# Attention, token mixing and FFT block: one product of zeros per attention step, theta's weights in two VectorE steps, mask copies and sink rows on GpSimd

## Chip, cores and metric

The kernel runs on one core of a Trainium2 chip. The metric is the device time of one execution in microseconds (us). The engines are TensorE (PE in the profile; PEld is its weight load), VectorE (DVE), ScalarE (ACT), GpSimd (POOL) and SyncE (SP, which here only issues DMAs). Each engine works through its own queue in order, and engines wait for each other by semaphores.

## The reference

Attention with a sliding window of 128 keys and 4 sink keys (2 batches, 8 heads, 768 positions, head size 64), then a block that turns each value by an angle and mixes the tokens, then a 2-D FFT's real part, a norm and an MLP. All inputs are f32.

```python
# attention, per batch and head; keep = first 4 keys, or the last 128 up to the query
a = softmax(where(keep, q @ k.T / 8, -1e9)); x = a @ v          # (2, 768, 512)
theta = x @ w_theta                                            # 512 x 512
zr, zi = x * cos(theta), x * sin(theta)
y = w_tok_r @ zr + w_tok_i @ zi                                # over the 768 tokens
u = x + y;  x = u + relu(u @ w_ch)
u = x + real(fft(fft(x, axis=1), axis=2))
out = u + relu(layernorm(u) @ w_ch1) @ w_ch2                   # 512 -> 2048 -> 512
```

The weights reach the kernel as 64-bit floating-point numbers, two 32-bit words each, and are converted to f32 on the chip.

## The kernel before

**Stages.** A first stretch (about 6 us) loads q, k, v and positions, and builds the first mask. Then comes attention (to about 140 us), token mixing of batch 0 and of batch 1 (`y_gen`), channel mixing and the Fourier transform (`ch_gen`, `dft_gen`), and the MLP in four chunks of three 128-row tiles (`mlp_gen`) to the end.

**Attention** (`attn_banded`) walks steps s. Tile n = s // 4 holds 128 queries of one batch, hp = s % 4 a pair of heads. At an even step the scores of four heads are multiplied (`score_mms`) and softmax runs on them (`scores`, L505): DVE adds the mask, writes scaled scores and the row minimum (L513), ACT takes the exponential (L517). The four score banks (tiles `sc` and `bank`) are reused by the next even step, so its products wait until ACT has read the last of them. One step later `turn` transposes the probabilities on PE (tile `tp`, L222), and ACT or DVE copies them to SBUF (L202, L203); three steps later `av` multiplies them by v (tile `oa`). `normalize` (L594 to L596) divides by the sums on DVE. From step 12 on, `theta_gen` multiplies a finished tile by theta's weights (tile `th`), 12 products a tile, spread over four steps; its end turns the result into a phase: ACT scales (L797), DVE rounds in two instructions (L798, L799), GpSimd subtracts (L800).

**Products of zeros.** In steps 1 to 11 (L630 to L638) PE multiplies a zero tile `z` into `th` twice per step; the results are not used.

**Masks** (`build_mask`, L415): `m0` to `m3` say what each kind of tile may see. Three DVE instructions per kind or fewer compute or copy them from the positions `win` (part of `xT`, which is reused later). `sink_v` (L468) spreads the sink rows of v over the heads, once per batch, on DVE.

**Conversion of weights** (`conv`, L263). A raw tile of 64-bit words arrives by DMA (three raw tiles, `raw`). ACT rescales the high words (L275). Then, if `low_act` is false, DVE works in three steps: shift the high word (L283), shift the low word and join (L284), put the sign in (L287). If `low_act` is true, ACT reduces the low word (L278) and DVE does two steps: L279 (shift and join) and L287. `low_act` is false until batch 1's token mixing and true after it. Theta's four weight tiles are converted in steps 5, 7, 9 and 11 (`THS`), and split into two f32r parts in steps 6, 8, 10 and 12 (ACT L202, GpSimd L207). From step 15 on the token-mixing weights follow (`P0B`).

**What sets the order.** The instructions are written in the order of the Python code, with hints such as "not before the last exponential" (`paced`, `after`). A scheduler with a simulated timeline then puts each engine's queue in order, so an edit in one place can move instructions in others.

Of the kernel before, what the change touches and what calls it, by code (L numbers as in the profile page):

```python
# [15 lines left out]
ALU = mybir.AluOpType  # L16
# [6 lines left out]
PW = 256 + SINK  # L23
BIG = 8.0e9
MAGIC = 12582912.0
# [17 lines left out]
P0B = 15  # L43
# [143 lines left out]
class _Body:  # L187
# [227 lines left out]
    def build_mask(self, n):  # L415

        nc, m = self.nc, self.masks
        win, key, sink = self.pos[:, 0:PW], self.pos[:, PW:PW + 128], self.pos[:, PW + 128:PW + 128 + SINK]
        a, s, z = slice(0, 128), slice(128, BLK), slice(BLK, PW)

        def drop(o, x, k):
            nc.vector.tensor_scalar(o, x, self.val[:, k:k + 1], -BIG, op0=ALU.is_ge, op1=ALU.mult)

        if n == 0:
            drop(key, key, 0)
            drop(win, win, 1)
            nc.vector.tensor_tensor(m[0], win[:, z], key, op=ALU.max)
        if n == 1:
            nc.vector.tensor_tensor(m[1][:, a], win[:, a], key, op=ALU.max)
            nc.vector.tensor_copy(m[1][:, 128:PW], win[:, 128:PW])  # L430
        if n == 2:
            drop(win[:, s], sink, 0)
            nc.vector.tensor_copy(m[2], win)
        if n == 3:
            for o, w in ((a, z), (s, s), (z, a)):
                nc.vector.tensor_copy(m[3][:, o], win[:, w])


    def pairs(self, what, n):
# [27 lines left out]

    def sink_v(self, b):  # L468
        vs = self.take(H, D)
        self.nc.vector.tensor_tensor(  # L470
            vs,
            self.ks[b][1].rearrange("p (o d) -> p o d", o=1).to_broadcast([128, H, D]),
            self.hm.rearrange("p (h o) -> p h o", o=1).to_broadcast([128, H, D]),
            op=ALU.mult,
        )
        self.vs[b] = vs
# [128 lines left out]
    def attn_banded(self):  # L605
        last = len(self.seq) - 1
        nc = self.nc
# [5 lines left out]
        for s in range(nstep + T0 + AL + 4):  # L613
# [16 lines left out]
            if 0 < s < first(0):  # L630

                ref = self.pe
                for _ in range(2):
                    i = nc.tensor.matmul(  # L634
                        self.zth[:, 0:256], lhsT=self.zz[:, 0:128], rhs=self.zz, start=s == 1, stop=False,
                        skip_group_check=True,
                    ).ins
                    self.after(i, ref)  # L638
# [24 lines left out]
            if n < last:  # L663
                if s in MST:
                    with self.paced(ref=self.last_exp):
                        self.build_mask(1 + MST.index(s))
                if s == SKS:
                    with self.paced(ref=self.last_exp):
                        self.sink_cols(0, 0, 1, 2)
                if hp == 0:  # L670
                    if n == 1:
                        with self.paced():
                            self.sink_v(0)
                    elif n and self.seq[n][1] == 0:
                        self.sink_cols(b, 0, 1)
                        self.sink_v(b)
            if s in THS:
                self.pump(0, lag=0, ref=self.last_exp)
            elif s - 1 in THS:
                with self.paced(ref=self.last_exp):  # L680
                    self.weight_split("th", THS.index(s - 1))
            elif P0B <= s < P0E and s % P0N == 0:
                self.pump(12, lag=0, ref=self.last_exp)
# [89 lines left out]
    def theta_gen(self, b, i):  # L773
        nc = self.nc
        x = self.x[b, i]
        tp = self.ps_tp.next().rearrange("p (a m) -> p a m", a=4)
        for a in range(4):
            self.tr(tp[:, a, :], x[:, a * 128:(a + 1) * 128], self.ident)
        hi = self.take(4, 128, dt=F32R)
        lo = self.take(4, 128, dt=F32R)  # L780
        self.rnd("a", hi, tp)
        xt = self.xT[b][:, :, i * 128:(i + 1) * 128]
        nc.scalar.activation(xt, tp, AF.Copy)
        self.low("v" if 6 * b + i >= ETH else "p", lo, xt, hi)
        self.tl = nc.cur_bb.bb.instructions[-1]
        yield
        th = self.ps_th.next()
        for a in range(4):
            wh, wl = self.ws["th", a]
            self.mm(th, hi[:, a, :], wh, a == 0, False)  # L790
            self.mm(th, hi[:, a, :], wl, False, False)
            self.mm(th, lo[:, a, :], wh, False, a == 3)
            if a < 3:
                yield
        self.give(hi, lo)
        ph, km = self.take(512), self.take(512)
        nc.scalar.activation(ph, th, AF.Copy, scale=INV2PI)  # L797
        nc.vector.tensor_scalar(km, ph, MAGIC, None, op0=ALU.add)  # L798
        nc.vector.tensor_scalar(km, km, MAGIC, None, op0=ALU.subtract)  # L799
        nc.gpsimd.tensor_tensor(ph, km, ph, op=ALU.subtract)  # L800
        self.give(km)
        self.ph[b, i] = ph
        yield
# [568 lines left out]
```

## Time and profile before

| what | value |
|---|---|
| median of 3 runs | 604.54 us (604.18 to 605.95) |
| the profiled execution | 604.34 us |
| its span in the trace | 602.6 us |
| PE busy | 587.1 us (97%) |
| DVE, ACT busy | 343.9 and 344.0 us (57% each) |
| POOL busy | 301.6 us (50%) |
| chain that ended last | PE 85%, DVE 8%, ACT 4% |

The span is what the trace covers; 1.7 us of the execution's time lie around it. Matmul ends are modelled, so PE's 97% means "something was always queued on PE", not that it worked at its peak. The chain that ended last follows the work back from the last instruction to what released it each time; an engine's share of it in a stretch says which engine the stretch waited for.

### The profile page before, as it was taken

To read this page: it belongs to the slowest core of one execution; us is meant where nothing else is said; L and a number is where in the kernel's file an instruction comes from. 1 tells how busy PE (TensorE), PEld (TensorE's weight loads), DVE (VectorE), ACT (ScalarE), POOL (GpSimd) and SP (SyncE) were. 2 spreads that over 40 slices of the span, in tenths; PEclk is the share of its full clock that TensorE was granted. 3 is DMA by queue.
4 is the path that set the end of the run, shared out by engine and by line. 5 is a ranking of instruction groups with operands and counts; after the bars stand their busy time and mean duration, and the time that the engine had idled before them with its cause. 6 is when DMAs were issued, how large, how long until landed. Compare 5 with 4: busy or idle time off the path is not lost.

```text
span 602.6 us, 9514 instructions
## 1 busy us (share of the span) xinstructions
PE 587.1 (97%) x3486; PEld 516.3 (86%) x3486; DVE 343.9 (57%) x711; ACT 344.0 (57%) x775; POOL 301.6 (50%) x252
## 2 busy tenths in 40 slices
PE   8989999999989999989999999999999999999996
PEld 6867888887878899968999999998998899998995
DVE  5776688868999678973566776465334211121112
ACT  4576666777864555556678784437447444344340
POOL 1121322144775542517655745659757565665651
PEclk9999999999999999999999999999999999999998
DMA  8842443200334314610066640100001000010001
GB/s 268 302 140 70 127 131 112 78 13 2 104 106 161 112 52 121 194 35 2 1 198 199 196 142 1 54 1 0 1 0 54 2 0 1 1 52 1 1 1 59
DMA packets 23336, 46.60 MB, mean 77 GB/s; under 512 B 2512, under 2 KB 9552, under 8 KB 23280
## 3 DMA queue, kind: packets, MB, share of 16 engines
q1 hardware_dynamic: 21744, 43.46, 22.8%
q0 software_dynamic: 1248, 2.17, 1.3%
q8 instruction: 29, 0.48, 0.3%
q10 hardware_dynamic: 288, 0.28, 0.1%
q14 instruction: 27, 0.22, 0.1%
HBM read 42.75 MB, written 3.15 MB: 76 GB/s over the span
## 4 chain that ended last, share of the span: by engine, by line
PE 85%; DVE 8%; ACT 4%; issue 1%; DMA 1%; POOL 1%; SPq 0%; ACTq 0%; DVEq 0%; POOLq 0%
PE pc L217 26%; PE acc L217 22%; PE s L217 9%; PE bank L217 8%; PE oa L217 6%; PE th L217 5%; PE tp L222 4%; PE sc L217 3%; PE s L222 2%; ACT t L202 1%; DVE t L207 1%; PE th L634 1%; ACT p L517 1%; DMA xT<-in_q_dram 1%; DVE t L818 1%
## 5 line engine op out<-in xcount | busy, mean ns | idle before, releaser
L207 POOL TENSOR_TENSOR t<-t 128x512 fp32r<-128x512 f32 x151 | 202.2, 1361 | 169.0 <-ACT t L202 143.6
L217 PE MATMUL acc<-t 128*128 128x512 f32 x648 | 178.5, 394 | 0.0
L202 ACT ACTIVATE t<-t 128x512 fp32r<-128x512 f32 x172 | 101.9, 625 | 71.5 <-PE acc L217 26.5
L217 PEld LDWEIGHTS acc<-t 128*128 128x128 f32 x648 | 116.5, 188 | 17.9
L217 PE MATMUL pc<-t 128*128 128x384 f32 (+1 forms) x672 | 124.8, 314 | 1.0 <-POOL t L207 0.6
L217 PEld LDWEIGHTS pc<-t 128*128 128x128 f32 x672 | 113.9, 188 | 10.9 <-POOL t L207 0.8
L1132 DVE SCALAR_TENSOR_TENSOR t<-pc,t 128x384 fp32r<-128x384 f32 x64 | 35.6, 557 | 123.4 <-ACT t L1131 122.1
L207 POOL TENSOR_TENSOR t<-xT,t 128x512 fp32r<-128x512 f32 x39 | 52.7, 1369 | 58.8 <-ACT t L202 27.2
L217 PE MATMUL s<-t 128*128 128x256 f32 (+3 forms) x492 | 70.6, 286 | 1.6 <-DVE st L1052 0.8
L217 PE MATMUL pc<-uh,t 128*128 128x384 f32 x256 | 70.6, 337 | 0.0
L217 PEld LDWEIGHTS s<-t 128*128 128x128 f32 x492 | 65.7, 190 | 5.0 <-DVE st L1052 1.0
L217 PE MATMUL bank<-t 128*128 128x512 f32 x216 | 65.7, 400 | 2.1 <-DVE t L207 1.6
L1131 ACT ACTIVATE t<-pc 128x384 fp32r<-128x384 f32 x64 | 31.3, 489 | 59.8 <-PE pc L217 57.1
L275 ACT ACTIVATE raw<-raw 128x512 f32<-128x512 f32 x58 | 38.9, 675 | 14.9 <-DMA raw<-in_w_ch_dram 13.2
L217 PEld LDWEIGHTS bank<-t 128*128 128x128 f32 x216 | 38.8, 188 | 9.6 <-DVE t L207 3.2
L217 PEld LDWEIGHTS pc<-uh,t 128*128 128x128 f32 x256 | 46.2, 188 | 0.8
L217 PE MATMUL pc<-ul,t 128*128 128x384 f32 x128 | 43.1, 336 | 0.6 <-DVE ul L207 0.6
L517 ACT ACTIVATE p<-sc,nb 128x272 f32<-128x272 f32 (+1 forms) x72 | 33.1, 466 | 15.4 <-DVE nb L513 14.9
L217 PE MATMUL oa<-t 128*128 128x64 f32 x288 | 39.3, 266 | 0.0
L217 PEld LDWEIGHTS oa<-t 128*128 128x128 f32 x288 | 37.2, 192 | 2.2 <-DVE t L203 0.7
L217 PE MATMUL th<-t 128*128 128x512 f32 x132 | 37.8, 416 | 0.0
L800 POOL TENSOR_TENSOR t<-t 128x512 f32<-128x512 f32 x12 | 17.1, 1421 | 36.9 <-DVE t L799 31.0
(145 smaller groups left out, 836.3 us busy)
## 6 DMA issues: line engine op xcount, KB each, us to landing
raw<-in_w_ch_dram SPq DMA_DIRECT2D x36, 512.0 KB, 4.2
kst<-in_k_dram SPq DMA_DIRECT2D x12, 256.0 KB, 4.0
raw<-in_w_tok_rT_dram SPq DMA_DIRECT2D x6, 512.0 KB, 3.5
raw<-in_w_tok_iT_dram SPq DMA_DIRECT2D x6, 512.0 KB, 3.6
out_dram<-t SPq DMA_DIRECT2D x12, 256.0 KB, 2.1
t<-in_q_dram SPq DMA_DIRECT2D x10, 256.0 KB, 5.1
t<-in_v_dram SPq DMA_DIRECT2D x10, 256.0 KB, 4.8
raw<-in_w_theta_dram SPq DMA_DIRECT2D x4, 512.0 KB, 6.5
```

The source lines that it names most:

```text
L202: return nc.scalar.activation(o, i, AF.Copy).ins
L207: e.tensor_tensor(o, x, hi.bitcast(F32), op=ALU.subtract)
L217: i = self.nc.tensor.matmul(o, lhsT=lhsT, rhs=rhs, start=start, stop=stop, skip_group_check=True).ins
L222: self.chained(self.nc.tensor.transpose(o, x, ident).ins)
L275: nc.scalar.activation(hf, hf, AF.Copy, scale=2.0 ** -112)
L517: self.last_exp = nc.scalar.activation(p[:, h, 0:wd], sc[:, 0:wd], AF.Exp, bias=nb[:, h:h + 1], scale=-1.0, accum_out=sm[:, h:h + 1]).ins
L634: i = nc.tensor.matmul(self.zth[:, 0:256], lhsT=self.zz[:, 0:128], rhs=self.zz, start=s == 1, stop=False, skip_group_check=True,).ins
L800: nc.gpsimd.tensor_tensor(ph, km, ph, op=ALU.subtract)
L818: self.tm = e.tensor_tensor(t, x, t, op=ALU.mult).ins
L1131: nc.scalar.activation(hh, hp, AF.Relu)
L1132: self.hl = nc.vector.scalar_tensor_tensor(hl, in0=hp, scalar=0.0, in1=hh.bitcast(F32), op0=ALU.max, op1=ALU.subtract).ins
```

## The change

- The loop that issues products of zeros runs once per step instead of twice: 11 products instead of 22.
- `low_act` is set to `s < P0B` in each attention step. P0B is 15, so theta's four weight tiles take the form with ACT's L278 and DVE's L279 and L287; the token weights from step 15 on are converted as before.
- The plain copies of the masks `m1`, `m2` and `m3` (five instructions) and both `sink_v` products go to GpSimd. The computed parts of the masks stay on DVE.
- The rounding of the phase, adding and subtracting MAGIC, becomes one DVE instruction (12 tiles).

```diff
@@ build_mask
-            nc.vector.tensor_copy(m[1][:, 128:PW], win[:, 128:PW])
+            nc.gpsimd.tensor_copy(m[1][:, 128:PW], win[:, 128:PW])
...
-            nc.vector.tensor_copy(m[2], win)
+            nc.gpsimd.tensor_copy(m[2], win)
...
-                nc.vector.tensor_copy(m[3][:, o], win[:, w])
+                nc.gpsimd.tensor_copy(m[3][:, o], win[:, w])
@@ sink_v
-        self.nc.vector.tensor_tensor(
+        self.nc.gpsimd.tensor_tensor(
@@ attn_banded
-                for _ in range(2):
+                for _ in range(1):
                     i = nc.tensor.matmul(
...
+            self.low_act = s < P0B
             if s in THS:
@@ theta_gen
-        nc.vector.tensor_scalar(km, ph, MAGIC, None, op0=ALU.add)
-        nc.vector.tensor_scalar(km, km, MAGIC, None, op0=ALU.subtract)
+        nc.vector.tensor_scalar(km, ph, MAGIC, MAGIC, op0=ALU.add, op1=ALU.subtract)
```

The scheduler's order changes in attention on PE, DVE, ACT, POOL and SP; behind the first third of batch 0's token mixing all queues of the executed branch stand in the same order as before. Lines behind L676 move down by one in the changed kernel (L797 becomes L798); the rounding keeps the number L799.

On DVE, at tile 1's second softmax and the first conversion of a theta weight (`raw_108`); `nb_172` and `sm_175` belong to tile 1, `nb_173` to tile 2. Before:

```order
L203 COPY t<-tp_199 128x256
L283 TENSOR_SCALAR t<-raw_108 128x512
L284 SCALAR_TENSOR_TENSOR t<-raw_108,t 128x512
L287 SCALAR_TENSOR_TENSOR t<-raw_108,t 128x512
L513 ISA sc_197,nb_172<-sc_197,m_187 128x272
L513 ISA nb_172 128x1
L513 ISA sc_196,nb_172<-sc_196,m_187 128x272
```

After:

```order
L203 COPY t<-tp_199 128x256
L279 SCALAR_TENSOR_TENSOR t<-raw_108 128x512
L513 ISA sc_197,nb_172<-sc_197,m_187 128x272
L513 ISA nb_172 128x1
L287 SCALAR_TENSOR_TENSOR t<-raw_108,t 128x512
L513 ISA sc_196,nb_172<-sc_196,m_187 128x272
```

One conversion step instead of three stands ahead of tile 1's second softmax.

On DVE, between tile 1's last and tile 2's first softmax, where the second theta weight (`raw_109`) is converted. Before:

```order
L594 TENSOR_SCALAR rs_178<-sm_175 128x8
L595 RECIPROCAL rs_178<-rs_178 128x8
L596 TENSOR_TENSOR t<-oa_200,rs_177 128x512
L203 COPY t<-tp_199 128x512
L283 TENSOR_SCALAR t<-raw_109 128x512
L284 SCALAR_TENSOR_TENSOR t<-raw_109,t 128x512
L513 ISA bank,nb_173<-bank,m_188 128x272
L513 ISA nb_173 128x1
L513 ISA sc_195,nb_173<-sc_195,m_188 128x272
```

After:

```order
L596 TENSOR_TENSOR t<-oa_200,rs_177 128x512
L203 COPY t<-tp_199 128x512
L594 TENSOR_SCALAR rs_178<-sm_175 128x8
L595 RECIPROCAL rs_178<-rs_178 128x8
L513 ISA bank,nb_173<-bank,m_188 128x272
L513 ISA nb_173 128x1
L513 ISA sc_195,nb_173<-sc_195,m_188 128x272
L513 ISA nb_173 128x1
L279 SCALAR_TENSOR_TENSOR t<-raw_109 128x512
L287 SCALAR_TENSOR_TENSOR t<-raw_109,t 128x512
```

The normalizing product L596 and the copy L203 no longer stand behind L594, which waits for the last exponential's sum, and the conversion has moved behind two of the four score instructions.

On ACT, the same place: the second theta weight between tile 1's and tile 2's exponentials. Before:

```order
L517 ACTIVATE p_184,sm_175<-bank,nb_172 128x272
L202 ACTIVATE t<-t 128x512
L275 ACTIVATE raw_109<-raw_109 128x512
L202 ACTIVATE t<-tp_198 128x512
L517 ACTIVATE p_183,sm_176<-bank,nb_173 128x272
```

After:

```order
L517 ACTIVATE p_184,sm_175<-bank,nb_172 128x272
L202 ACTIVATE t<-t 128x512
L275 ACTIVATE raw_109<-raw_109 128x512
L278 ACTIVATE raw_109<-raw_109,below 128x512
L202 ACTIVATE t<-tp_198 128x512
L517 ACTIVATE p_183,sm_176<-bank,nb_173 128x272
```

L278 is new there, ahead of the copy and of the next four exponentials.

## Rows read from the trace of the kernel before

**Rows 1.** Stages: start:end, length, each engine's busy us, PE's granted clock, DMA.

```profile
5.00:21.00 16.00, 15.11 (x102) 11.75 (x103) 11.72 (x54) 10.19 (x42) 0.30 (x1) 1.00 1.00 351
21.00:38.00 17.00, 15.56 (x117) 12.71 (x113) 14.60 (x42) 9.67 (x32) 3.52 (x3) 1.00 0.58 182
...
80.00:133.00 53.00, 53.00 (x370) 42.55 (x370) 40.32 (x131) 38.77 (x122) 15.89 (x13) 1.00 0.25 79
133.00:180.00 47.00, 44.86 (x264) 37.65 (x263) 43.75 (x58) 35.99 (x63) 29.71 (x20) 1.00 0.22 68
```

**Rows 2.** Chain shares by line, 21 to 38 us, then 80 to 133 us.

```profile
by line: ACT p L517 16.1%; DVE t L283 13.3%; DVE sc L513 12.4%; DVE t L284 12.3%; DVE t L203 10.5%; issue 7.4%; DVE t L596 7.3%; DVE t L287 6.6%; DVE bank L513 4.2%; DVE t L470 4.0%; ACT raw L275 3.4%; ACT t L202 3.1%; DVE nb L513 2.9%; DVE
...
by line: PE oa L217 30.9%; PE th L217 27.3%; PE tp L222 20.7%; PE sc L217 15.0%; PE bank L217 6.3%
```

**Rows 3.** Products of zeros: ns min/median/max, first and last start.

```profile
L634 PE MATMUL th<-z x44: 379/379/483, 6.6 to 30.8; 128*128 128x256 f32 x44
```

**Rows 4.** Chain in order of time: start us, us, what.

```profile
6.87 1.52 ACT p L517 x8
...
13.03 1.06 PE th L634 x4
```

**Rows 5.** First theta load: issue in the timeline, then us to landing.

```profile
8.79 1.31 SPq L251 DMA_DIRECT2D raw<-in_w_theta_dram  x3
...
raw<-in_w_theta_dram SPq DMA_DIRECT2D x1, 512.0 KB, 6.1
```

**Rows 6.** Timeline, 15 to 36 us: start, us, engine, what, [idle before].

```profile
15.01 0.67 ACT L275 ACTIVATE raw<-raw 128x512 f32<-128x512 f32 x1
...
17.52 0.44 DVE L513 CUSTOM_DVE_ANT_0 sc<-sc,m 128x272 f32<-128x272 f32 x1
...
21.00 0.59 ACT L202 ACTIVATE t<-tp 128x512 f32<-128x512 f32 x1
...
22.89 0.44 DVE L513 CUSTOM_DVE_ANT_0 bank<-bank,m 128x272 f32<-128x272 f32 x1
...
23.49 0.49 ACT L517 ACTIVATE p<-bank,nb 128x272 f32<-128x272 f32 x1 [1.90 <-DVE nb L513]
...
25.79 0.63 ACT L202 ACTIVATE t<-t 128x512 fp32r<-128x512 f32 x1
...
26.50 1.27 POOL L207 TENSOR_TENSOR t<-t 128x512 fp32r<-128x512 f32 x1 [4.53 <-ACT t L202]
...
27.01 1.04 DVE L283 TENSOR_SCALAR t<-raw 128x512 int32<-128x512 int32 x1 [1.31 <-ACT raw L275]
...
30.62 0.49 ACT L517 ACTIVATE p<-sc,nb 128x272 f32<-128x272 f32 x1 [3.16 <-DVE nb L513]
...
35.94 0.49 ACT L517 ACTIVATE p<-bank,nb 128x272 f32<-128x272 f32 x1 [1.57 <-DVE nb L513]
```

**Rows 7.** The two-step conversion where it runs later: L278 and L279.

```profile
L278 ACT ACTIVATE raw<-raw,below x33: 734/754/784, 205.8 to 360.9; 128x512 int32<-128x512 uint32 x33
...
L279 DVE SCALAR_TENSOR_TENSOR t<-raw x9: 676/685/1799, 206.6 to 252.7; 128x512 int32<-128x512 int32 x9
```

**Rows 8.** DVE instructions that the change removes or moves, by line.

```profile
L798 DVE TENSOR_SCALAR t<-t x12: 410/425/925, 46.2 to 166.9; 128x512 f32<-128x512 f32 x12
...
L470 DVE TENSOR_TENSOR t<-vsr,hm x2: 681/682/684, 11.5 to 29.4; 128x512 f32<-128x512 f32 x2
...
L433 DVE COPY m<-xT x1: 295/295/295, 10.3 to 10.3; 128x272 f32<-128x272 f32 x1
```

**Rows 9.** Timeline of DVE in batch 0's token mixing.

```profile
162.94 1.78 DVE L287 SCALAR_TENSOR_TENSOR t<-raw,t 128x512 int32<-128x512 int32 x1
...
166.95 0.93 DVE L798 TENSOR_SCALAR t<-t 128x512 f32<-128x512 f32 x1
```

**Rows 10.** The last microseconds, columns as in rows 1.

```profile
598.00:600.00 2.00, 0.00 (x0) 0.00 (x0) 0.00 (x0) 0.00 (x0) 0.00 (x0) 0.67 0.61 220
600.00:601.00 1.00, 0.00 (x0) 0.00 (x0) 0.00 (x0) 0.00 (x0) 0.00 (x0) 0.50 0.07 20
```

## The prediction, made before the changed kernel ran

> **What bounds the kernel now.** I read the windows of the stages first, then the chain that ended last inside each, and only then single rows. The stages show four regimes. In the opening of attention (5 to 21 us) the DMA engines are busy all the time (share 1.00) and PE is busy as well, but part of that is products of zeros. From 21 to 38 us VectorE is the fullest engine, 14.60 of 17 us, and the chain there is made of exponentials and of VectorE's conversion steps L283, L284 and L287; matmuls hardly stand in it [rows 1, 2]. From 80 to 133 us the chain is PE alone. From 133 to 180 us, the turn to token mixing, VectorE is busy 43.75 of 47 us and PE waits for it [rows 1, 2]. Behind that PE sets the end, and all queues stand in the same order before and after. So a change in the first 180 us shifts what follows as a whole: what attention and the turn gain, the end gains.
>
> **Term A: attention's opening, to 36 us.** Two things are removed here, products of zeros and VectorE work, and one is added on ScalarE.
>
> A product of zeros is two matmul rows (44 rows for 22 products), and a pair of products takes 1.06 us of the chain [rows 3, 4]. Halving them frees 11 x 0.53 = 5.8 us on PE if PE were what everything waits for. It is not. The first group stands beside eight exponentials that hold the chain for 1.52 us [rows 4], so nothing comes of it. Later groups are on the chain until tile 1 (13.03 us), and PE gets about 1.6 us ahead by its second scores. But then the queues meet the first theta load, which no product of zeros moves: issued at 8.79 us, 6.1 us to landing, so it lands at 14.9 us, and ACT's L275 started on it at 15.01 us [rows 5, 6]. So I follow ACT and DVE from that landing, by four points.
>
> Point 1, the second softmax of tile 1 on DVE, at 17.52 us before [rows 6]. In the new order one conversion step stands ahead of it, not three, but L278 stands ahead of that. From 14.9 us: L275 0.67, L278 0.75, L279 0.69, with 0.1 for signals, gives 17.1 us [rows 6, 7]. That is 0.4 earlier; the 1.6 us of PE are cut to this.
>
> Point 2, the first exponential of tile 2, at 23.49 us before, 1.90 us of it spent waiting for DVE, which had L594 to L596, a copy, L283 and L284 ahead of its L513 at 22.89 [rows 6]. In the new order L596 and the copy no longer stand behind L594's wait, and L279 stands behind two of the score instructions. So ACT is what remains. Its queue is as before with one L278 more: the copy that began at 21.00 begins at 21.00 - 0.4 + 0.75 = 21.35, takes 0.59, and the exponential comes at 22.0. That is 1.5 earlier.
>
> Point 3, the second softmax of tile 2, exponential at 30.62 us before, after waiting 3.16 us [rows 6]. ACT takes 2.3 us from its first exponential to the next L202 (23.49 to 25.79). So 22.0 + 2.3 = 24.3, then L202 0.63, L275 0.67, L278 0.75 give 26.35, L279 0.69 gives 27.05, and a score instruction and its exponential (0.6, from 22.89 to 23.49) 27.7. That is 2.9 earlier. It contains sink_v's 0.68 us on DVE, which stood here ahead of the scores [rows 8], and the slow L283 of 1.04 us [rows 6].
>
> Point 4, tile 3's first exponential, at 35.94 us before. From 27.7: 2.3 for the exponentials, 0.63 + 0.67 + 0.75, and two copies of at most 0.59 give 33.2, that is 2.7 earlier; one L283 less among the scores behind it makes about 0.3 more. **A = -3.0 us.**
>
> Bounds of A. The far end is PE's, -5.8. The near end comes from GpSimd. The mask copies cost DVE at most 0.30 us each and sink_v 0.68 us [rows 8]; what they cost on GpSimd no row shows, and the nearest row is a product of the same size, 1.27 us [rows 6]. Nobody waits for them directly: the masks m2 and m3 are first used by tile 2 and later (behind 20 us), m1 at 12 us. But they run beside DVE. An L283 that began while GpSimd's product of 26.50 us ran took 1.04 us, and in token mixing an L287 took 1.78 us where its like takes 0.69 [rows 6, 7, 9]. If both sink_v products hit a conversion step like that, 2 x 1.1 = 2.2 us come back and A is -0.8. I take -3.0, since the copies fall into 6 to 12 us, ahead of the conversions, and only one sink_v meets them.
> The Trainium skill speaks against the move here: SBUF — State Buffer, section "Who interferes with whom", says that GpSimd and VectorE share a pair of ports, and that when VectorE reads two tensors from SBUF, or runs in its mode with both ports, whichever comes second waits for the first to finish. The rows just named agree; by that rule every one of the seven moved instructions may stop VectorE once, and A would be the -0.8 of the near end.
>
> **Term B: attention from 36 to 133 us.** Eight of the twelve roundings lie here, 0.42 us each on DVE [rows 8], and the scheduler has set score products ahead of theta's products in several places, which gives softmax more cover. The chain is PE alone [rows 2], and PE's work is the same, so I book nothing: **B = 0**. For bounds I take the weight load's idle time, 53 - 42.55 = 10.5 us [rows 1]: PE's rows hide waits in there, a fifth of which may be won or lost by a new order, so -2 to +2.
>
> **Term C: the turn to token mixing, 133 to 180 us.** DVE is full here and PE waits for its splits. Two roundings' first halves (L798) lie in the full stretch, a usual one of 0.42 us and one stretched to 0.93 us [rows 8, 9], and the queues around them are unchanged, so what is taken out comes off the end of the stretch: **C = -1.3 us**. Bounds: 0, if GpSimd's products then meet DVE elsewhere; -2.2, with two more roundings in the 133 to 143 us tail.
>
> **Sum.** -3.0 + 0 - 1.3 = -4.3 us. The profiled execution took 604.34 us (span 602.6 and 1.7 around it), so the changed one takes 600.0; the median of the runs stands 0.2 above the profiled execution: **600.2 us**. The bounds together give 604.34 - 9.9 to 604.34 + 1.2; they will not all fall to one side.
>
> **Rivals.**
> 1. More than forecast: the new order lets PE run closer to its own work in attention (B = -2), or A comes nearer to PE's end. Then about 597. For it: softmax has more cover in the new order. Against: the chain names nothing but PE. Chance 0.13.
> 2. The gain is covered: the conversions on ACT and DVE, with GpSimd in the way, hold the opening (A = -0.8). With B and C that gives 604.5 - 2.1 = 602.4. For it: the added L278 stands ahead of exponentials four times, 3.0 us of ACT. Against: ACT is busy 9.67 of 17 us in 21 to 38 [rows 1]. Chance 0.15. This is also the case in which the removed products do nothing, since PE then waits for softmax instead.
> 3. The lead is given back: attention ends 3 us earlier, but in a worse order, and C's stretch begins with another GpSimd and DVE overlap (A + B = 0). Then 603.2. Chance 0.12.
> 4. Slower: TensorE's clock. The granted clock is 1.00 in every stage [rows 1]; that is the 2.4 GHz level. It falls only behind the last matmul, with PE at rest, to 0.67 and then to 0.50, the 1.2 GHz level [rows 10]. The products of zeros fill pauses of PE, and half of them go. If the clock fell for the stretch from 15 to 35 us, PE's work there (15.56 us busy of 17, less 4 x 0.53 of zeros, about 13.4 per 17 us [rows 1, 4]) would run at half speed, so 20 us of it lose 10, and the sum is -4.3 + 10: 610. It decides from about 9 us at the low level on, where half of the time lost eats the gain. Against: PE still has work in four fifths of the time. Chance 0.10.
> The Trainium skill has this as a rule, TensorE: Matmul & The Clock Gate, section "HAM oscillation — how this bites in real kernels": pauses of PE bring its clock to half, and the products behind each pause start slow. The trace agrees at its end and shows no fall inside the program.
>
> **How the numbers follow.** My forecast, 598.3 to 602.3, has 0.50; rivals 1 to 4 have 0.13, 0.15, 0.12 and 0.10. The range leaves out rival 4 and the lower half of rival 1: 596.5 to 604.2. What a measurement of this kernel can tell from no change is about 0.3%, 1.8 us, so faster means below 602.7. The forecast, rival 1 and most of rival 2 are faster: 0.50 + 0.13 + 0.09 = 0.72. The rest of rival 2, and rival 3 but for 0.01, are the same: 0.17. Rival 4 and that 0.01 are slower: 0.11.
>
> **What would show it.** Point by point in the changed trace: the first L275 still near 15 us (if earlier, the load was not what held it); the second softmax of tile 1 near 17.1, the exponentials of points 2 to 4 near 22.0, 27.7 and 33.2; PE in the same order of work about 3 us earlier at 80 to 133 us; the end of DVE's full stretch about 4.3 us earlier, near 175 instead of 180; from there on the same distances as before. I am wrong on A if those exponentials move by under 1 us or by over 5, on B if the lead at 133 us differs from that at 36 us by over 2 us, on C if it does not grow by about 1 us to 180 us, and wholly if the granted clock shows a stretch below 1.00 ahead of the end.

## The result, and the profile after

The changed kernel takes 599.91 us (median, 599.74 to 600.28) against 604.65 us (604.18 to 605.95): a ratio of 0.9917 [0.9905, 0.9929], so 4.7 us or 0.8% faster. The forecast of 600.2 us lies 0.3 us off, and the gain is well beyond the 0.3% that a measurement can tell. The profiled execution took 599.92 us, 4.4 less than the one before.

The stage windows of the changed kernel, which answer to [rows 1] (start:end, length, busy us of PE, PEld, DVE, ACT, POOL, then PE's granted clock, DMA share, GB/s):

```profile
5.00:21.00 16.00, 14.11 (x91) 9.58 (x89) 10.97 (x47) 10.73 (x42) 2.77 (x7) 1.00 0.99 353
21.00:38.00 17.00, 16.15 (x130) 13.61 (x130) 13.33 (x44) 14.30 (x45) 6.33 (x5) 1.00 0.65 219
...
80.00:133.00 53.00, 52.61 (x370) 43.11 (x369) 34.86 (x113) 36.73 (x112) 15.49 (x13) 1.00 0.21 66
133.00:180.00 47.00, 46.06 (x265) 38.99 (x264) 42.49 (x59) 32.79 (x60) 28.55 (x19) 1.00 0.24 74
```

In the first stage PE is busy 1.0 us less. In the second DVE falls from 14.60 to 13.33 us and ACT rises from 9.67 to 14.30. In the last DVE falls from 43.75 to 42.49 and PE rises from 44.86 to 46.06. The granted clock is 1.00, the 2.4 GHz level, in all four.

The four points of term A, from the timeline of the changed kernel; they answer to [rows 6]:

```profile
15.14 0.68 ACT L275 ACTIVATE raw<-raw 128x512 f32<-128x512 f32 x1
15.70 0.75 ACT L278 ACTIVATE raw<-raw,below 128x512 int32<-128x512 uint32 x1
...
16.48 0.70 DVE L279 SCALAR_TENSOR_TENSOR t<-raw 128x512 int32<-128x512 int32 x1 [1.76 <-ACT raw L278]
...
17.10 0.44 DVE L513 CUSTOM_DVE_ANT_0 sc<-sc,m 128x272 f32<-128x272 f32 x1
...
22.20 0.50 ACT L517 ACTIVATE p<-bank,nb 128x272 f32<-128x272 f32 x1
...
28.09 0.49 ACT L517 ACTIVATE p<-sc,nb 128x272 f32<-128x272 f32 x1 [0.77 <-DVE nb L513]
...
32.89 0.50 ACT L517 ACTIVATE p<-bank,nb 128x272 f32<-128x272 f32 x1
```

Forecast were 17.1, 22.0, 27.7 and 33.2; the lead over the kernel before is 0.4, 1.3, 2.5 and 3.05 us. The waits at points 2 and 3, 1.90 and 3.16 us before, are gone and 0.77 us. Times count from the first instruction of each execution; the first exponential of all comes at 6.87 us before and at 7.30 us after, so a few tenths between two executions say little.

The end of attention and the end of DVE's full stretch are read on PE: the first product into `pc` opens the long run of token mixing, and a matmul of L217 into `bank` gets the last split that comes late (the second part of a value, made by DVE's L207). First the kernel before, then the changed one, both from the timeline:

```profile
150.03 0.52 PE L217 MATMUL pc<-t 128*128 128x256 f32 x3
...
179.69 0.51 PE L217 MATMUL bank<-t 128*128 128x512 f32 x1 [1.15 <-DVE t L207]
```

```profile
146.55 0.52 PE L217 MATMUL pc<-t 128*128 128x256 f32 x3
...
175.38 0.50 PE L217 MATMUL bank<-t 128*128 128x512 f32 x1 [0.28 <-DVE t L207]
```

The lead is 3.5 us at the first of the two places and 4.3 us at the second, as summed. In between it is not steady. The first exponential of a softmax comes 4.2 us earlier at 36.4 us, 9.9 earlier at 69.1 and 6.4 earlier at the last softmax (122.1). The last product of attention with the sink rows (PE, into `oa`) comes only 2.4 earlier, at 142.86 instead of 145.28, but there the order differs: six products into `bank` stand ahead of it, not two, so it is no measure of PE's lead. So the numbers fit; whether the reasons do is what the experiments ask.

### The profile page after: what moved, and what is told of

It reads as the page before. It is cut to its first block, busy times and chain, and to the rows that moved or that the text cites. A ratio compares the mean times of both kernels' runs of the same rounds, so it can differ in the third digit from the quotient of the medians.

```text
span 598.1 us, 9446 instructions
## 1 busy us (share of the span) xinstructions
PE 583.1 (97%) x3464; PEld 512.8 (86%) x3464; DVE 332.8 (56%) x688; ACT 344.0 (58%) x779; POOL 305.4 (51%) x259
## 4 chain that ended last, share of the span: by engine, by line
PE 63%; DVE 5%; ACT 1%; POOL 1%; issue 1%; POOLq 0%; ACTq 0%
PE pc L217 25%; PE acc L217 21%; PE s L217 9%; PE bank L217 7%; PE s L222 2%; POOL t L207 1%; DVE t L207 1%; ACT t L202 1%; DVE t L1145 0%; DVE t L818 0%; DVE t L986 0%; DVE t L998 0%; DVE t L1001 0%; ACT t L1067 0%; DVE t L1052 0%
## 5 line engine op out<-in xcount | busy, mean ns | idle before, releaser
L207 POOL TENSOR_TENSOR t<-t 128x512 fp32r<-128x512 f32 x151 | 203.3, 1366 | 151.5 <-ACT t L202 124.6
L217 PE MATMUL acc<-t 128*128 128x512 f32 x648 | 178.5, 394 | 0.0
L217 PEld LDWEIGHTS acc<-t 128*128 128x128 f32 x648 | 116.5, 188 | 17.9
L217 PE MATMUL pc<-t 128*128 128x384 f32 (+1 forms) x672 | 124.9, 314 | 1.0 <-POOL t L207 0.6
L217 PEld LDWEIGHTS pc<-t 128*128 128x128 f32 x672 | 113.9, 188 | 10.9 <-POOL t L207 0.8
L207 POOL TENSOR_TENSOR t<-xT,t 128x512 fp32r<-128x512 f32 x39 | 52.4, 1362 | 47.6 <-ACT t L202 27.6
L217 PE MATMUL s<-t 128*128 128x256 f32 (+3 forms) x492 | 70.5, 286 | 1.6 <-DVE st L1052 0.8
L217 PE MATMUL pc<-uh,t 128*128 128x384 f32 x256 | 70.6, 337 | 0.0
L217 PEld LDWEIGHTS s<-t 128*128 128x128 f32 x492 | 65.9, 190 | 4.9 <-DVE st L1052 1.0
L217 PE MATMUL bank<-t 128*128 128x512 f32 x216 | 65.1, 398 | 0.9 <-DVE t L207 0.9
L275 ACT ACTIVATE raw<-raw 128x512 f32<-128x512 f32 x58 | 39.2, 679 | 16.4 <-DMA raw<-in_w_ch_dram 8.4
L217 PEld LDWEIGHTS pc<-uh,t 128*128 128x128 f32 x256 | 46.2, 188 | 0.8
L800 POOL TENSOR_TENSOR t<-t 128x512 f32<-128x512 f32 x12 | 18.1, 1508 | 56.1 <-DVE t L799 51.2
L217 PEld LDWEIGHTS bank<-t 128*128 128x128 f32 x216 | 38.7, 188 | 7.7 <-DVE t L207 2.0
L217 PE MATMUL pc<-ul,t 128*128 128x384 f32 x128 | 43.1, 336 | 0.6 <-DVE ul L207 0.6
L217 PE MATMUL oa<-t 128*128 128x64 f32 x288 | 38.4, 265 | 0.0
L217 PE MATMUL th<-t 128*128 128x512 f32 x132 | 37.4, 415 | 0.2 <-POOL t L207 0.2
L217 PEld LDWEIGHTS oa<-t 128*128 128x128 f32 x288 | 37.0, 193 | 0.4
```

The costliest lines, as they stand in the source:

```text
L207: e.tensor_tensor(o, x, hi.bitcast(F32), op=ALU.subtract)
L217: i = self.nc.tensor.matmul(o, lhsT=lhsT, rhs=rhs, start=start, stop=stop, skip_group_check=True).ins
L275: nc.scalar.activation(hf, hf, AF.Copy, scale=2.0 ** -112)
```

## The experiments

Four explanations compete for the 4.7 us. The conversion: ACT's L278 takes work off DVE, as the prediction's points 1 to 4 have it. PE's time: the products of zeros were on the path after all. Order: the scheduler lays out the queues anew. The clock: shorter fillers lower it. Each part was made alone and undone alone, then single causes were taken apart. All of these kernels do the whole computation, since the products of zeros enter no result.

**The parts alone, on the kernel before.** First one product of zeros per step, not two:

```diff
-                for _ in range(2):
+                for _ in range(1):
```

> The kernel before with only the products of zeros halved. Conversion theory (the opening is held by the theta load, then by ACT and DVE): PE gets ahead by up to 1.6 us by tile 1 but meets the L275 that waits for the load, so the time falls by at most 0.5 us, to about 604.2, and tile 2's first exponential stays within 0.5 us of 23.5. PE theory (PE is what everything waits for to the end of attention): 11 x 0.43 = 4.7 us less, about 600. Order theory (the scheduler's new order decides, not the part): anything, with exponentials that move where no part of the change stands.

Measured: 603.04 us (601.5 to 606.3), ratio 0.9971 [0.9961, 0.9982]. Its granted clock differs from run to run: with a mean of 0.997 or more it took 601.5 to 602.7, with 0.994 to 0.996 it took 602.9 to 603.6. The profiled run took 606.32 at 0.990, and its windows show where the clock went (columns as above):

```profile
28.00:32.00 4.00, 2.40 (x17) 1.47 (x17) 3.97 (x14) 2.48 (x10) 0.00 (x0) 1.00 0.46 149
32.00:36.00 4.00, 4.00 (x22) 3.20 (x19) 3.46 (x11) 2.77 (x10) 1.27 (x1) 0.53 0.22 64
36.00:40.00 4.00, 4.00 (x21) 3.74 (x22) 0.94 (x3) 1.49 (x6) 1.27 (x1) 0.50 0.46 135
40.00:44.00 4.00, 4.00 (x25) 3.04 (x22) 1.81 (x8) 2.81 (x9) 0.18 (x1) 0.69 0.39 125
```

PE was busy 2.40 of 4 us from 28 to 32, then ran at the 1.2 GHz level for about 10 us. Without such a fall this one part gives 1.8 to 3.0 us, more than the 0.4 that the prediction booked for it; in the median half of that is lost.

The two-step conversion alone:

```diff
+            self.low_act = s < P0B
```

> The kernel before with only theta's weights converted in the two-step form. Conversion theory: about 3.0 us less, near 601.6, tile 2's second softmax about 2.5 and tile 3's first exponential about 2.5 to 3 us earlier. PE theory: no change beyond 0.5 us, since PE's work is the same. Order theory: anything between.

Measured: 604.01 us (603.5 to 604.5), ratio 0.9987 [0.9977, 0.9996]: 0.5 us. The exponentials of the four points come at 18.4, 23.4, 30.4 and 36.0 us, where the kernel before has 18.1, 23.5, 30.6 and 35.9. The order of the queues nearly stays. What the prediction made the source of the 3 us is worth a sixth of it by itself.

The rounding alone:

```diff
-        nc.vector.tensor_scalar(km, ph, MAGIC, None, op0=ALU.add)
-        nc.vector.tensor_scalar(km, km, MAGIC, None, op0=ALU.subtract)
+        nc.vector.tensor_scalar(km, ph, MAGIC, MAGIC, op0=ALU.add, op1=ALU.subtract)
```

> The kernel before with only the rounding in one DVE instruction. My term C: 1.3 us less, near 603.3, all of it won between 133 and 180 us, attention up to 133 us unchanged. PE theory: 0. Order theory: attention's exponentials move by more than 0.5 us although eight roundings of 0.42 us lie beside PE's work there.

Measured: 605.65 us (604.8 to 606.8), ratio 1.0013 [1.0002, 1.0024]: 1.1 us slower, with less work in it. PE's queue stands in another order, and the first product into `pc` comes at 152.10 us, not 150.03. From there to the matmul that has the last late split in the kernel before it takes 28.4 us, not 29.7: the turn gains, and attention loses more.

The GpSimd moves alone (three of its four changed lines are shown, `m3` is left out):

```diff
-            nc.vector.tensor_copy(m[1][:, 128:PW], win[:, 128:PW])
+            nc.gpsimd.tensor_copy(m[1][:, 128:PW], win[:, 128:PW])
...
-            nc.vector.tensor_copy(m[2], win)
+            nc.gpsimd.tensor_copy(m[2], win)
...
-        self.nc.vector.tensor_tensor(
+        self.nc.gpsimd.tensor_tensor(
```

> The kernel before with only the mask copies and the sink rows on GpSimd. Conversion theory: DVE loses one 0.68 us product ahead of tile 2's second softmax, so up to 0.7 us less (603.9); if GpSimd's products block DVE instead, up to 2.2 us more (606.8). PE theory: 0.

Measured: 605.59 us (603.9 to 607.3), ratio 1.0013 [0.9996, 1.0029]: no gain. Half of its runs show a mean clock of 0.995 and take 605.9 to 607.3.

The four parts alone add up to -1.5 - 0.5 + 1.1 + 1.1 = +0.2 us; together they give -4.7. They are not separate terms.

**The parts undone, on the changed kernel.** The zeros back (`range(2)`), the other three parts kept:

> The changed kernel with two products of zeros per step again. Runs so far at an undisturbed clock: zeros alone -3.0 us, conversion alone -0.5, rounding alone +0.8, GpSimd alone -0.3. If the parts add, the three without the zeros give about 604.5, the time before. If the conversion is worth the 1.1 us that taking it out of the changed kernel cost, and rounding and GpSimd the 0.6 and 0.5 likewise, 602.3. The queue of PE is then neither kernel's (232 places from the one before, 542 from the changed one).

Measured: 605.57 us (604.8 to 607.4), ratio 1.0017 [1.0007, 1.0027]. Without the halved zeros the change is no gain at all. PE's order is nearly that of the rounding alone, and so is the time (605.65 us): in this order the conversion and the GpSimd moves add nothing.

The old conversion back (the line with `low_act` out):

> The changed kernel with theta's weights converted in three VectorE steps again. Its order of instructions is the changed kernel's (PE's queue differs in 8 places, the kernel before's in 542). Conversion theory (my term A): the second softmax of tile 2 and tile 3's first exponential come about 2.5 us later, and the time goes to about 602.9. Order theory (the new order of the queues, set off by the halved zeros, is what gains): the time stays within 0.7 us of 599.9, as long as the granted clock stays at 1.00. Clock theory: pauses of PE get longer than in the changed kernel, the granted clock falls for a stretch between 15 and 45 us as in the run with the zeros alone, and some runs are 2 to 5 us slower.

Measured: 601.10 us (600.8 to 602.4), ratio 0.9932 [0.9908, 0.9956]. The order is the changed kernel's. Its timeline at points 3 and 4:

```profile
28.34 0.49 ACT L517 ACTIVATE p<-sc,nb 128x272 f32<-128x272 f32 x1 [2.38 <-DVE nb L513]
...
32.95 0.49 ACT L517 ACTIVATE p<-bank,nb 128x272 f32<-128x272 f32 x1 [0.84 <-DVE nb L513]
```

ACT waits for DVE here as it did before, 2.38 us, and yet the exponentials come 0.25 and 0.06 us behind the changed kernel's. At point 2 the old conversion is even 0.95 us ahead (21.25 against 22.20), with no L278 in ACT's queue, and by point 3 that is lost. The leads of the four points don't come from the conversion. It wins 0.8 us at tile 3's second softmax (37.2 against 36.4) and 1.2 us at the end.

The two-instruction rounding back:

> The changed kernel with the rounding in two VectorE instructions again. My term C: 1.3 us more, 601.2, lost between 133 and 180 us. Order theory: the queues become nearly those of the run with the zeros alone, whose fastest runs took 601.6, so 601 to 602, with a lead that is the same in attention's opening and differs behind it.

Measured: 600.74 us (600.1 to 602.8), ratio 0.9937 [0.9912, 0.9962]. The profiled execution took 600.10, and its stretch ends at 175.66 us against 175.38. So within the change the rounding is worth 0.2 to 0.8 us. The order of attention changes with it: the first product into `pc` comes at 146.18 us, 0.37 ahead of the changed kernel's, and from there to the last late split it takes 29.5 us, not 28.8.

The copies and the sink product back on DVE:

> The changed kernel with mask copies and sink rows on VectorE again; PE's and ACT's queues stay as they are (2 and 0 places). My price: DVE gets back 0.7 us ahead of tile 2's second softmax and about 1.1 us of copies in 6 to 12 us, so 600.3 to 600.9. If GpSimd's products were in DVE's way: 0.5 to 2 us less, 598 to 599.4. Order theory: within 0.4 us of 599.9.

Measured: 602.89 us (600.0 to 604.2), ratio 0.9947 [0.9927, 0.9967]. Two runs with a mean clock of 0.999 took 600.0 and 600.8, the others, at 0.991 to 0.996, 601.2 to 604.2. The order is the changed kernel's. The windows of its profiled run (603.45 us):

```profile
20.00:24.00 4.00, 3.50 (x16) 2.46 (x16) 3.28 (x10) 3.80 (x12) 1.27 (x1) 0.54 1.07 321
24.00:28.00 4.00, 4.00 (x20) 2.98 (x21) 1.39 (x6) 2.13 (x6) 0.38 (x1) 0.61 0.92 337
```

So the move to GpSimd is worth 0.1 to 0.9 us where the clock holds, and some 3 us in the median, because it does hold with it. Its own cost is seen in the changed kernel, from the timeline, and behind it the same instruction with the product on DVE (the kernel of this experiment):

```profile
11.24 1.03 POOL L470 TENSOR_TENSOR t<-vsr,hm 128x512 f32<-128x512 f32 x1
11.30 1.00 DVE L594 TENSOR_SCALAR rs<-sm 128x8 f32<-128x8 f32 x1 [0.73 <-ACT p L517]
```

```profile
11.12 0.17 DVE L594 TENSOR_SCALAR rs<-sm 128x8 f32<-128x8 f32 x1 [0.17 <-ACT p L517]
```

An instruction on 8 columns takes as long as the GpSimd product that it began beside. The first softmax of tile 1 on DVE starts at 12.75 us, against 12.21 with the product on DVE: 0.5 us, 0.2 of it a later start of the execution. At the second softmax nothing of it is left: 17.10 against 17.66, since L275 waits for its load in the kernel with the product on DVE.

**No product of zeros at all** (`range(0)` in the changed kernel):

> The changed kernel with no products of zeros in attention's steps at all (the output is not touched by it); the queues are otherwise the changed kernel's. PE theory: 11 x 0.43 = 4.7 us less once more, about 595.2. Conversion theory: nothing, 599.9 within 0.5, since PE only waits longer for softmax. Clock theory: the granted clock falls in the opening of attention, to 1.2 GHz for a stretch of 10 to 30 us between 12 and 45 us, and the time rises by 3 to 8 us, to 603 to 608.

Measured: 602.82 us (601.8 to 607.5), ratio 0.9983 [0.9954, 1.0013]. The mean clock is 0.979 to 0.992 in all runs. Two windows of the profiled one:

```profile
8.00:12.00 4.00, 3.78 (x20) 2.93 (x21) 2.08 (x11) 3.10 (x17) 1.19 (x3) 0.50 1.00 298
...
24.00:28.00 4.00, 4.00 (x25) 4.00 (x24) 1.25 (x7) 3.46 (x11) 1.24 (x1) 0.50 0.85 300
```

The windows of this execution add up to some 13.7 us at the low level (0.95, 0.50 and 0.70 from 4 to 16 us, 0.65, 0.50 and 0.99 from 20 to 32 us), and it took 1.9 us more than the changed kernel's. If half of the 13.7 us was lost, as in the falls below, the removed products gave 4.9 us. That is an estimate; no run shows this kernel at an undisturbed clock. What is shown is that the clock falls without the products of zeros, and that the kernel is then slower.

**Zero columns apart from order, as far as it went.** Two products of half the width, in the changed kernel. PE's queue stands nearly as with the zeros back (6 places differ), its columns of zeros are those of the changed kernel:

```diff
-                for _ in range(1):
+                for _ in range(2):
...
-                        self.zth[:, 0:256], lhsT=self.zz[:, 0:128], rhs=self.zz, start=s == 1, stop=False,
+                        self.zth[:, 0:128], lhsT=self.zz[:, 0:128], rhs=self.zz[:, 0:128], start=s == 1, stop=False,
```

> The changed kernel with two products of zeros of 128 columns per step in place of one of 256: the same columns, but the order of the changed kernel with both products of zeros (PE's queue differs from that one's in 6 places, from the changed kernel's in 542). PE-time theory: 599.9, as the changed kernel. Order theory: as the changed kernel with its zeros back, 602 to 604.5, and tile 2's first exponential as late as there.

Measured: 602.64 us (602.0 to 603.7), ratio 0.9968 [0.9951, 0.9984], clock 1.00 throughout. Against the zeros back, in nearly the same order of PE, that is -2.9 us; to the changed kernel, with the same columns, another -2.7 us are left. Groups of zeros in the timeline, with the zeros back (start us, us; this execution took 607.38 us, with a fall of the clock behind the lines shown):

```profile
17.70 1.13 PE L634 MATMUL th<-z 128*128 128x256 f32 x4
...
21.97 1.13 PE L634 MATMUL th<-z 128*128 128x256 f32 x4
24.92 1.08 PE L634 MATMUL th<-z 128*128 128x256 f32 x4
28.19 1.13 PE L634 MATMUL th<-z 128*128 128x256 f32 x4
30.29 1.08 PE L634 MATMUL th<-z 128*128 128x256 f32 x4
```

and the same groups at half the width:

```profile
16.24 0.71 PE L634 MATMUL th<-z 128*128 128x128 f32 x4
...
22.34 0.66 PE L634 MATMUL th<-z 128*128 128x128 f32 x4
23.97 0.66 PE L634 MATMUL th<-z 128*128 128x128 f32 x4
26.82 0.71 PE L634 MATMUL th<-z 128*128 128x128 f32 x4
28.51 0.66 PE L634 MATMUL th<-z 128*128 128x128 f32 x4
```

A group is 0.42 us shorter. The lead is 1.5 us at the first of these groups. At tile 2's first scores it is cut to 0.57 us (20.28 against 20.85), since they wait for a softmax, much as predicted. The second group is no measure: with half products it stands behind eight products into `oa`, with the zeros back ahead of them. From the third on the lead is 0.95, 1.4 and 1.8 us, so each group adds its 0.42, and the first exponential of tile 3 comes at 33.4 against 36.1.

DVE's order is not the same either. With the zeros back the normalizing product L596 stands behind L594:

```profile
20.49 0.17 DVE L594 TENSOR_SCALAR rs<-sm 128x8 f32<-128x8 f32 x1 [0.86 <-ACT p L517]
...
20.82 0.64 DVE L596 TENSOR_TENSOR t<-oa,rs 128x512 f32<-128x512 f32 x1
```

and with half products it stands ahead of L594, as in the changed kernel:

```profile
19.33 0.69 DVE L596 TENSOR_TENSOR t<-oa,rs 128x512 f32<-128x512 f32 x1
...
20.53 0.16 DVE L594 TENSOR_SCALAR rs<-sm 128x8 f32<-128x8 f32 x1
```

So the -2.9 us hold PE's time and this piece of order together; how much the piece gives was not measured.

The other 2.7 us are order. In the changed kernel, behind the second scores of tile 2:

```profile
35.08 0.99 PE L217 MATMUL sc<-kst,t 64*128 64x288 f32 x5
...
36.25 0.66 PE L222 MATMUL tp<-ident,t 128*128 128x128 f32 x4
36.41 0.49 ACT L517 ACTIVATE p<-sc,nb 128x272 f32<-128x272 f32 x1 [0.84 <-DVE nb L513]
...
39.90 0.49 PE L217 MATMUL sc<-kst,t 64*128 64x272 f32 x1
...
41.01 2.37 PE L217 MATMUL th<-t 128*128 128x512 f32 x9
```

and with two half products:

```profile
35.77 0.66 PE L222 MATMUL tp<-ident,t 128*128 128x128 f32 x4 [0.65 <-DVE t L203]
36.74 0.99 PE L217 MATMUL sc<-kst,t 64*128 64x288 f32 x5
...
38.07 0.49 ACT L517 ACTIVATE p<-sc,nb 128x272 f32<-128x272 f32 x1 [0.53 <-DVE nb L513]
...
40.55 2.54 PE L217 MATMUL th<-t 128*128 128x512 f32 x10
...
43.47 0.49 PE L217 MATMUL sc<-kst,t 64*128 64x272 f32 x1
```

Here the four transposes wait 0.65 us for DVE's copy and the scores stand behind them, so the exponential of tile 3's second softmax comes 1.66 us later; and ten products of theta stand ahead of the next tile's scores, which the changed kernel has ahead of them. The first product into `pc` comes at 149.40 us, 2.85 later.

**Shorter filler in the kernel before.** The kernel before with three products of 64 columns in place of two of 256, in nearly its own order (26 places of PE's differ):

```diff
-                for _ in range(2):
+                for _ in range(3):
...
-                        self.zth[:, 0:256], lhsT=self.zz[:, 0:128], rhs=self.zz, start=s == 1, stop=False,
+                        self.zth[:, 0:64], lhsT=self.zz[:, 0:128], rhs=self.zz[:, 0:64], start=s == 1, stop=False,
```

> The kernel before, with three products of zeros of 64 columns per step in place of two of 256: about half of their time on PE, in nearly the order of the kernel before (PE's queue differs in 26 places, ACT's in 2). PE-time theory (the zeros gain by the time that PE gets back): as the zeros alone at an undisturbed clock, 601.5. Order theory (they gain by the order that the scheduler then makes): 604.5 within 0.7. Either may lose 1 to 5 us where the granted clock falls between 16 and 45 us.

Measured: 612.96 us (612.7 to 613.1), ratio 1.0141 [1.0119, 1.0163]: 8.5 us slower. From its windows:

```profile
24.00:28.00 4.00, 4.00 (x29) 4.00 (x28) 2.92 (x11) 2.14 (x9) 0.00 (x0) 0.64 0.91 308
28.00:32.00 4.00, 4.00 (x20) 2.95 (x18) 2.97 (x5) 1.53 (x3) 1.27 (x1) 0.50 0.05 18
...
40.00:44.00 4.00, 4.00 (x22) 4.00 (x22) 1.98 (x9) 2.78 (x10) 1.14 (x1) 0.50 0.42 131
44.00:48.00 4.00, 4.00 (x17) 2.85 (x18) 1.06 (x5) 1.66 (x5) 1.40 (x2) 0.50 0.20 66
```

Taking a window's clock as a mix of the two levels, and with 1.2 and 1.0 us from the windows at 36 and 48 us (0.85 and 0.87), it ran 2.9 + 4.0 + 1.2 + 8.0 + 1.0 = 17.1 us at the low level. Half of that is 8.5, but the fit is not clean. Tile 2's first exponential is late before the clock can have done it; it comes at 23.49 us in the kernel before:

```profile
25.86 0.49 ACT L517 ACTIVATE p<-bank,nb 128x272 f32<-128x272 f32 x1 [3.69 <-DVE nb L513]
```

PE's clock is below 1.00 only behind 24 us, and DVE has an L283 of 1.10 us at 21.73 us ahead of L596, which the kernel before has the other way round. These 2.4 us were there ahead of any fall, with another order on DVE, and what the shorter products saved on PE counts against the loss: a group takes 0.88 us at 16.70 us where the kernel before has 1.13 at 17.45, so it is not the half that was expected. So the clock has the greater part in the 8.5 us, not all of it, and the run does not decide between PE's time and order.

**The theta load issued earlier.** The prediction had L275 held by the first theta load. In the changed kernel, with the first two theta loads issued two steps sooner (the first at 6.98 us, where it was 8.78; 0.7 us of that is an earlier start of this execution):

```diff
-AH = 5
+AH = 3
```

> The changed kernel with the first theta loads called for two steps earlier (AH 3, not 5): the queues of PE, ACT and DVE are the same in every place, on SP two theta loads move ahead of tile 2's third load of k, q and v. The first theta load then lands near 13.5 us, not 15. If the landing holds L275 in the changed kernel: up to 1 us less, 599. In its profile ACT was busy until 15.05 and L275 began at 15.14, so I expect 599.4 to 599.9, with less scatter; if the k, q and v behind it come late instead, 600 to 602.

Measured: 599.60 us (599.2 to 600.3), ratio 0.9924 [0.9902, 0.9946], not to be told from the changed kernel's. The timeline has L275 right behind the exponentials of tile 1's first softmax, as the changed kernel has:

```profile
14.33 0.21 ACT L517 ACTIVATION_READ_ACCUMULATOR p<-sc,nb 128x1 f32 x1
14.42 0.67 ACT L275 ACTIVATE raw<-raw 128x512 f32<-128x512 f32 x1
```

It begins 0.72 us earlier, but so does everything in this execution: the first exponential of all to L275 is 7.8 us in both. ACT's own queue holds L275, not the load.

## Why the prediction held, and which steps of it did not

**The total** is right to 0.3 us and the four points to 0.4; the reason given for them is not. Two steps failed, a third was mis-sized, and their errors cancel: that the total fits so well is luck.

**Step "halving the zeros is not on the path" failed.** It was booked at 0.4 us, since the theta load would cut PE's lead. The load holds L275 with the zeros halved alone, with the copies back on DVE, with two half products and with the short ones (waits of 0.79, 0.97, 0.19 and 0.49 us); in the changed kernel L275 waits for no load, and with the load issued earlier the changed kernel stays at its time. The cut itself is real, but it is at tile 2's first softmax, and I stopped counting there. Four more groups of zeros run from there on; the lead is 1.8 us at the last of them and 2.7 at 33 us. The halved columns, with the piece of DVE's order that came with them, are worth 2.9 us (605.57 to 602.64). The size per group was off too: 0.43 us (1.08 to 1.13 us before, 0.65 to 0.70 after), not 0.53: a group of half the products takes more than half as long. The "eight exponentials" beside the first group are four, each with a read of its sum; nothing hangs on that.

**Step "the conversion gives the -3.0" failed.** It was worked out exactly from durations (L278 0.75 and L279 0.69 were right), and points 2 to 4 came within 0.4 us, but the kernel with the old conversion reaches points 3 and 4 within 0.25 us of the changed one as well, and point 2 earlier. The conversion is worth 0.5 us alone and 1.2 in the change. Following one queue from a fixed point gave the right time for a thing that another queue had made early: point 2 leaned on an order in which L596 and the copy no longer stood ahead of the scores, and that order came with the halved zeros: the zeros halved alone have it too, with L596 at 19.34 us and L594 at 20.54, and the conversion alone does not (20.74 and 20.42).

**Term B, 0 as booked, was right at its end alone.** By my own measure, the lead at 133 us against that at 36, the softmaxes say 6.4 (at 122) against 3.05 us at point 4: more than the 2 us that I had named as its refutation. The new order runs scores early and theta's products late, so the softmaxes lead by up to 10 us and PE's own work by much less: 3.5 us at the first product into `pc`. Only that lead reaches the turn, and by it the 0 stands.

**Term C, -1.3 us, was over-sized; its mechanism was right.** The stretch's end moved as summed (175.38; forecast 175.4), but the lead grows by only 0.8 us in the turn, from 3.5 at the first product into `pc` to 4.3, and the wait at the last late split falls from 1.15 to 0.28 us. DVE's busy time fell by 1.26 us there, and not all of it was waited for. What is missing is the bound that I had named, GpSimd's products meeting DVE elsewhere: the rounding of 0.93 us and the 0.42 of the other half are one instruction of 0.41 us at 163.09, but the L207 just behind it takes 1.41 us at 164.02, where it took 0.68 at 168.39 before: GpSimd's L800, which the rounding releases, runs beside it from 163.58 us for 1.30. Undoing the rounding makes the turn 0.65 us longer (29.5 against 28.8), while undoing the conversion leaves it as it is: the conversion's 0.8 us (176.18 against 175.38) are there at the turn's beginning (147.37 against 146.55). So A and B together gave about 3.5 us and C 0.8, where 3.0 and 1.3 were booked. The bounds of the sum add to -10.0 us, not -9.9; nothing hangs on that either.

**GpSimd.** Blocking of VectorE was in the bounds of A, and among the moved instructions it is seen at one place (1.00 us instead of 0.17), of which nothing is left at 17 us; the near end, -0.8, did not come. The Trainium skill's rule in SBUF — State Buffer, section "Who interferes with whom", that the second to issue waits for the first to finish, agrees with that instruction: it ends at 12.30 us, the product on GpSimd at 12.27. The moved copies, 0.20 to 0.42 us, left no trace on the path. That the move would matter through the clock was in no term.

**Rivals 1 to 3.** Neither the covered gain nor the lead given back came. Rival 1's mechanism, a better order, is where 2.7 us come from, but inside the forecast's total and not on top of it. They are counted against the order of two products with the new rounding, which is itself worse than the order before (605.65 against 604.5 us).

**Rival 4, the clock,** did not come true: 1.00 up to the end. But it was near, in several of the partial changes. Its price was right: about half of the time at the low level is lost where two executions of one kernel are compared. With the zeros halved alone it is 10.2 us (windows 0.53, 0.50, 0.69) for 606.3 - 601.5 = 4.8; with the copies back 6.8 us (0.54, 0.61) for 603.45 - 600.0 = 3.45; with the zeros back 3.4 us (0.75 and 0.82 from 36 to 44 us) for 607.4 - 605.6 = 1.8 against the median. The Trainium skill's TensorE: Matmul & The Clock Gate, section "HAM oscillation — how this bites in real kernels", names this danger for pauses of PE. The falls here come behind waits of PE of 0.5 to 2.2 us, but the kernel before has one of 1.05 us at 38.27 and the changed kernel one of 0.85 us at 30.64, and neither falls, so the runs bear out the danger and do not say which waits bring it.

**The accounts, then:** the three other parts without the zeros +1.1 us (604.47 to 605.57), the halved columns of zeros -2.9, and the order that comes with a single product -2.7: -4.5 in all, where 4.6 were measured against the 604.47 of those runs.

**What stays open.** Why the scheduler chooses the better order with one product and the worse with two or with the new rounding alone was not followed. No kernel had the better order together with the longer zeros, so the split into -2.9 and -2.7 is measured along one path only, and a piece of DVE's order is in the -2.9. And why the clock holds in the changed kernel, but falls in most executions with five copies and two products moved back to DVE, isn't settled; only where it falls and what that costs.

## What to carry to other kernels

Work that waits are filled with is not free because one wait swallows its saving: follow the saving past that point, group by group, to the next place where everything meets. Where a scheduler sets the order, no edit is a separate term: a part made alone can lose and still help in the whole, so make each part alone and also undo it, and compare the queues before the times. Whoever shortens filler on TensorE should look at the granted clock of each stretch in several executions, since about half of the time at the low level was lost here.

## What the runs showed of the hardware that I had not expected

- Shorter filler in the pauses of PE can make the kernel slower than longer filler: with three products of 64 columns instead of two of 256 the time rose by 8.5 us, some 2.4 of them ahead of any fall, with the clock at the low level for 6.9 and then 10.2 us. Without any filler the mean clock is down in every execution, and the kernel takes 2.9 us more than with one product per step.
- A VectorE instruction on 128x8 took 1.00 us, not 0.17, beside a GpSimd product of 1.03 us, and 0.90 us beside another of 1.30 us at 39.40 us in the changed kernel.
- The sink product, 0.68 us on VectorE, takes 1.03 and 1.55 us on GpSimd (the second began 0.04 us behind a VectorE instruction of 0.69 us); a mask copy of 128x272 takes 0.41 us instead of 0.30.
- The same work in another order of the queues differed by 2.7 us of 600, nearly as much as halving the columns of zeros gave (2.9).
